# Sending the expert gates of twenty chunks through DRAM in transposed form, inside a fused attention and mixture-of-adapters kernel

## The chip, the cores and the metric

The kernel runs on one NeuronCore of one Trainium2 chip. The metric is the device time of one execution in microseconds, as the median of repeated runs. A separate execution was taken by the hardware profiler; its own time and its span are given below, and every duration quoted from a row or a trace is from that one execution.

The engines are TensorE (PE, with its weight loads shown apart as PEld), VectorE (DVE), ScalarE (ACT), GpSimd (POOL) and SyncE (SP). SP computes nothing here: it only issues DMAs, in program order. POOL also issues one kind of DMA, the query casts.

## The reference

Attention over spatially pooled keys feeds a top-2 mixture of low-rank adapters, applied to every token:

```
kv_pool = kv.reshape(B, H//4, 4, W//4, 4, C).mean(axis=(2, 4))   # 768 keys per batch
k = v = kv_pool.reshape(B, -1, C) @ w_sr
x = softmax(q @ k.T / sqrt(C)) @ v          # B = 4, 12288 queries each, C = 128
logits = x @ w_gate                         # 8 experts
w = softmax over the two largest logits of each token, 0 for the other six
out = x + sum over experts e of  w[e] * ((x @ A[e]) @ B[e])      # rank 16
```

The eight adapters together are one 128x128 matrix on the way down (8 experts times rank 16) and one on the way up. The gate of an expert multiplies its 16 rank columns between the two.

## The kernel before, in words

The 49152 tokens are cut into 96 chunks of 512 (24 chunks per batch), and four chunks make a group that shares one query load. Inside a chunk, S = 4 blocks of 128 tokens are handled side by side. All engines run from one order written by hand: the start and the last 24 chunks are literal lists of steps, and chunks 14 to 71 come from `slot(k)`, which emits the steps of one slot. Each engine executes its own instructions strictly in that order, so the place of a step in a slot is also its place in the engine's queue.

A chunk passes through a slot pipeline. In slot k:

- `sc k 0..2` computes the scores of chunk k, three times two 128x512 matmuls, and ACT takes the exponential of each pair (`em`).
- `at k-1 0..3` multiplies chunk k-1's exponentials with the values: four blocks of six matmuls into `acc`. The values carry the gate logits and a row sum as extra columns.
- `nm k-2` (DVE: reciprocal, then one multiply) normalizes into `xn`; `tp k-2` takes the sorted top logits (four MAX8); `ro` lets POOL work out the tanh argument and the top-2 mask for a pair of chunks.
- `ga k-4`, once per pair: ACT's tanh, then two POOL operations give the gates `gw` of both chunks, laid out tokens by experts.
- `tt k-6 k-7`: eight 128x128 transposes on PE into one PSUM tile, four of them of chunk k-6's normalized output, four of chunk k-7's gated product `hg`; one DVE copy brings all eight to SBUF (`tts`).
- `dn k-6`: four 128-column matmuls with the transposed output as weights give the down projection with tokens on partitions, and `ge k-6` multiplies it by `gw` on DVE, which expands each gate over its 16 rank columns in the access pattern.
- `up k-8`, `fi k-8`: the up projection from the transposed `hg`, the addition of the attention output on DVE, and the output DMA on SP.

Other work is laid in between: `pr` and `pa` prepare the keys and values of the next batch (PE and DVE in `pr`, POOL in `pa`), `kv` loads it (SP), `lq` (SP) loads the transposed queries of a group by a DMA transpose, and `cq` (POOL) casts a later group's queries to bf16 from DRAM to DRAM. `lq` must wait for its cast. `cq` begins with a one-element copy `late` that reads the previous group's `qT`, so a cast does not start before that load has landed.

PSUM is fully used: `sg` two buffers of two banks, `acc` one of two banks, and `mb` two buffers of one bank that `tt`, `dn`, `up` and `pr` take in turn.

The lines that matter in the profile: line 68 is the helper that records every matmul, line 79 the cast, line 84 the DMA transpose, 319 the exponential, 333 and 337 the normalization, 367 the MAX8, 380 to 386 the routing, 392 to 395 the gates, 416 the copy after the transposes, 430 the gate product, 443 and 444 the addition and the output DMA, 606 the `late` copy.

Of the kernel before, what the change touches and what calls it, by code (L numbers as in the profile page):

```python
# [10 lines left out]
FP32 = mybir.dt.float32  # L11
BF16 = mybir.dt.bfloat16
U16 = mybir.dt.uint16
FP16 = mybir.dt.float16
AF = mybir.ActivationFunctionType
ALU = mybir.AluOpType
# [4 lines left out]
def kernel(  # L21
# [10 lines left out]
    nc = tc.nc  # L32
    P = 128
    B, N, C = q.tensor.shape
    E, RK = 8, 16
# [3 lines left out]
    T = 512  # L39
    S = T // P  # L40
    GC = 4
    GT = GC * T
# [6 lines left out]
    const = ctx.enter_context(tc.tile_pool(name="const", bufs=1))  # L49
# [6 lines left out]
    rpool = ctx.enter_context(tc.tile_pool(name="rpool", bufs=4))  # L56
    gpool = ctx.enter_context(tc.tile_pool(name="gpool", bufs=6))
    run = ctx.enter_context(tc.tile_pool(name="run", bufs=3))
    opool = ctx.enter_context(tc.tile_pool(name="opool", bufs=6))
    qdram = ctx.enter_context(tc.tile_pool(name="qdram", bufs=1, space=bass.MemoryType.DRAM))  # L60
    ps_s = ctx.enter_context(tc.tile_pool(name="ps_s", bufs=2, space=bass.MemoryType.PSUM))
    ps_a = ctx.enter_context(tc.tile_pool(name="ps_a", bufs=1, space=bass.MemoryType.PSUM))
# [2 lines left out]
    keep = tc.keep_in_program_order  # L65

    def mm(*a, **k):
        return keep(nc.tensor.matmul(*a, **k))  # L68

    def mtile(shape, dtype=FP32, name="mb"):  # L70
        return ps_m.tile(shape, dtype, tag="mb", name=name)


    NG = N // GT
    q_bf, qT, kvr = {}, {}, {}

    def cast_q(g):
        t = qdram.tile([GT, C], BF16, tag=f"q{g}", name=f"qbf{g}")
        keep(nc.gpsimd.dma_start(t, q[g // NG, (g % NG) * GT:(g % NG + 1) * GT]))
        q_bf[g] = t  # L80

    def load_qT(g):
        t = qpool.tile([P, GT], BF16, tag="qT", name="qT")
        keep(nc.sync.dma_start(t.rearrange("c (j p) -> c j p", p=P),
                               q_bf[g].rearrange("(p j) c -> p (j c)", p=P), transpose=True))
        qT[g] = t


# [34 lines left out]
    for item in """  # L123
# [5 lines left out]
        at = [None if x == "-" else int(x) for x in at]  # L129
# [13 lines left out]
    id_f = const.tile([P, P], FP32)  # L143
# [24 lines left out]
    def one(pool):  # L168
        if pool == "mb":
            return mtile([P, T], name="tail_ps")  # L170
        if pool == "acc":
            return ps_a.tile([P, S, 256], FP32, tag="acc", name="acc").rearrange(
                "p a c -> p (a c)")[:, 0:T]
        return ps_s.tile([P, 2, T], FP32, tag="sg", name="sg")[:, 0]

    def move(engine, o, i):
        return keep(nc.scalar.copy(o, i) if engine == "A" else nc.vector.tensor_copy(o, i))
# [129 lines left out]
    em, acc, xn, xg, srt, gw = {}, {}, {}, {}, {}, {}  # L307
    tts, xT, hgT, hp, hg, dp = {}, {}, {}, {}, {}, {}
# [34 lines left out]
    def normalize_half(k, h):  # L343
        if ("r", k) not in xn:
            xn["r", k] = rpool.tile([P, S], FP32, tag="rinv", name="rinv")
        if k // GC not in xg:
# [5 lines left out]
            xn[k][:, 2 * h:2 * h + 2], a[:, :, 0:VC],  # L352
            ri.unsqueeze(2).broadcast_to([P, 2, VC]), op=ALU.mult)))

    sizes = [1, 1] + [2] * (NB * (B - 1) // 2 - 1) + [1] * NB
    first, size = {}, {}
    for n in sizes:
        k0 = len(first)
# [3 lines left out]
    def top(k):  # L362
        k0, m = first[k], k - first[k]
        if k0 not in srt:
            srt[k0] = rpool.tile([P, GC, S, 8], FP32, tag="srt", name="srt")
        for s in range(S):
            keep(nc.vector.max(srt[k0][:, m, s], xn[k][:, s, C:VC]))  # L367

# [2 lines left out]
    def route(k0):  # L371
        n = size[k0] * S
        eng = nc.gpsimd
        m0 = k0 % GC * S
        lg = xg[k0 // GC].rearrange("p m s c -> p (m s) c")[:, m0:m0 + n, C:VC]
        so = srt[k0].rearrange("p m s e -> p (m s) e")[:, 0:n]

        def over(i):
            d = rpool.tile([P, GC * S, 8], FP32, tag=f"over{i}", name=f"over{i}")[:, 0:n]
            keep(eng.tensor_tensor(  # L380
                d, lg, so[:, :, i].unsqueeze(2).broadcast_to([P, n, 8]), op=ALU.subtract))
            return d

        arg, mask = over(0), over(1)
        keep(eng.tensor_tensor(arg, arg, mask, op=ALU.add))  # L385
        keep(eng.tensor_scalar(mask, mask, 0.0, None, op0=ALU.is_ge))  # L386
        routed[k0] = (n, eng, arg, mask)

    def gates(k0):
        n, eng, arg, mask = routed[k0]  # L390
        th = rpool.tile([P, GC * S, 8], FP32, tag="th", name="th")[:, 0:n]
        keep(nc.scalar.activation(th, arg, AF.Tanh, bias=0.0, scale=0.5))  # L392
        w = gpool.tile([P, GC * S, 8], FP32, tag="gw", name="gw")
        keep(eng.tensor_tensor(w[:, 0:n], th, mask, op=ALU.mult))  # L394
        keep(eng.tensor_tensor(w[:, 0:n], w[:, 0:n], mask, op=ALU.add))
        gw[k0] = w
# [30 lines left out]
    def gate(k):  # L427
        k0, m = first[k], k - first[k]
        hg[k] = run.tile([P, S, P], BF16, tag="hg", name="hg")
        keep(nc.vector.tensor_tensor(  # L430
            hg[k].rearrange("p s (e r) -> p (s e) r", e=E),
            hp[k].rearrange("p s (e r) -> p (s e) r", e=E),
            gw[k0][:, m * S:(m + 1) * S].rearrange("p s e -> p (s e)")
            .unsqueeze(2).broadcast_to([P, S * E, RK]), op=ALU.mult))

    def up(k):
        dp[k] = mtile([P, S, C], name="d_ps")
        for s in range(S):
            mm(dp[k][:, s], hgT[k][:, s], b_bf, start=(s == 0), stop=(s == S - 1))
# [153 lines left out]
    a_bf = const.tile([P, P], BF16)  # L593
    b_bf = const.tile([P, C], BF16)

    def adapters():
        keep(nc.vector.tensor_scalar(a_bf, a_f, 0.5, None, op0=ALU.mult))
        keep(nc.vector.tensor_copy(b_bf, b_f))

    def first_casts(watch):  # L600
        keep(nc.gpsimd.tensor_copy(late, watch))
        for g in range(2, 4):
            cast_q(g)

    def next_cast(g):
        keep(nc.gpsimd.tensor_copy(late, qT[g - 1][:, 0:1]))
        cast_q(g)
# [3 lines left out]
    def plan(b):  # L611
# [8 lines left out]
        "k2": project_k, "va": project_v, "vb": copy_v, "tu": turn_v,  # L620
        "cs": lambda w: first_casts(q_f[1][:, 15, 0:1]),
        "cab": adapters,
        "lq": load_qT, "cq": next_cast,
        "kv": lambda b, h, r: load_kv(b, h, r, None),
        "pa": lambda b, n: plan(b)[0][n // 8][n % 8](),
        "pr": lambda b, n: plan(b)[1][n](),
        "sc": scores, "at": attend, "nm": normalize, "tp": top, "ro": route, "ga": gates,
        "tt": lambda x, h, e: transposes(x, h, nc.scalar if e == "A" else nc.vector),
        "dn": down, "up": up,
        "ge": lambda k: gate(k) if len(hp[k].shape) == 3 else gate_part(k, 0, S),  # L630
        "fi": lambda k: finish(k) if len(dp[k].shape) == 3 else add_here(k, 0, S),
        "nh": normalize_half, "xb": hold_x, "xt": turn_x, "cx": fetch_x, "hb": hold_h, "ht": turn_h, "ch": fetch_h,
        "o95": hold_acc, "pt": attend_part, "hd": hold_hp, "dn2": down_into, "ge2": gate_part,
        "db": hold_d, "up2": up_part, "af": add_here, "ca": carry, "pd": add_there,
        "lastroute": route_here, "lt": tanh_here, "lg_": gates_here,
    }

    def follow(order):
# [7 lines left out]
    def slot(k):  # L646
        b, i = divmod(k, NB)
        o = []
        if k % GC == 0 and k // GC + 1 < B * NG:
            o.append(f"lq {k // GC + 1}")  # L650
        i0 = 4 if b == 0 else 0
        if b + 1 < B and i0 <= i < i0 + 12:
            o.append(f"kv {b + 1} {(i - i0) // 4} {(i - i0) % 4}")
        if k % GC == 2 and k // GC + 2 < B * NG:
            o.append(f"cq {k // GC + 2}")
        o.append(f"sc {k} 0")
        if first[k - 4] == k - 4:
            o.append(f"ga {k - 4}")
        o += [f"nm {k - 2}", f"tt {k - 6} {k - 7} V", f"sc {k} 1", f"up {k - 8}", f"fi {k - 8}",
              f"at {k - 1} 0", f"tp {k - 2}"]  # L660
        if first[k - 2] + size[k - 2] - 1 == k - 2:
            o.append(f"ro {first[k - 2]}")
        o += [f"sc {k} 2", f"dn {k - 6}", f"ge {k - 6}"]
        prs = (14, 15, 16, 18, 19, 20, 21, 22, 23) if b == 0 else (11, 12, 13, 17, 18, 19, 21, 22, 23)
        if b + 1 < B and i in prs:
            o.append(f"pr {b + 1} {prs.index(i)}")
        o += [f"at {k - 1} {s}" for s in range(1, S)]
        if b + 1 < B and i % 2 == 0 and (8 if b == 0 else 6) <= i <= 20:
            lo, n = ((0, 3, 7, 10, 14, 17, 21)[(i - 8) // 2], 4 if i % 4 else 3) if b == 0 else (
                (i - 6) // 2 * 3, 3)  # L670
            o += [f"pa {b + 1} {m}" for m in range(lo, lo + n)]
        return "; ".join(o)
# [119 lines left out]
```

The softmax here doesn't subtract the row's maximum and nothing guards it: scores larger than these inputs give would overflow.

## Time and profile before

| | us |
|---|---|
| median of 9 runs | 389.12 (389.03 to 389.47) |
| the profiled execution | 389.18 |
| its span | 387.4 |
| PE busy in the span | 374.4 (97%) |
| DVE busy | 313.5 (81%) |
| ACT busy | 308.5 (80%) |
| POOL busy | 211.4 (55%) |

The granted TensorE clock is full in all 40 slices of the span. A slot of the loop lasts about 3.6 us, longer where `pr` adds its matmuls; slot 34 begins at 142.30 us of the span, slot 36 at 149.83, slot 40 at 164.99. Busy time of PE is modelled from pipelined matmuls, so 97% by itself does not say how close PE is to its peak; the order of the matmuls in time does.

### The profile page before, as it was taken

The page shows a single profiled execution, that of the slowest core. Times are in us where ns is not written, and L with a number is a line of the kernel's source. Part 1 is how long each engine was busy: PE and PEld are TensorE (multiplying, and loading weights), DVE is VectorE, ACT ScalarE, POOL GpSimd, SP SyncE. Part 2 cuts the span into 40 slices and gives each one's busy share as a digit, 9 for nine tenths or more (in the row PEclk, how much of TensorE's full clock was granted, in tenths as well). Part 3 has the DMA queues.
Part 4 walks back from the last instruction along what each step waited for, and adds up shares of the span by engine and source line. Part 5 has one row for each costly group of instructions (what it writes and reads, how often), then busy time and mean ns, then how long its engine had stood idle before and what let it go on. Part 6 is the DMA issues. An engine that isn't in the chain of part 4 may idle for free.

```text
span 387.4 us, 11738 instructions
## 1 busy us (share of the span) xinstructions
PE 374.4 (97%) x4546; PEld 303.6 (78%) x4620; DVE 313.5 (81%) x973; ACT 308.5 (80%) x401; POOL 211.4 (55%) x474
## 2 busy tenths in 40 slices
PE   7999999999999999999999999999999999999994
PEld 4867888888888888888888888888877778788893
DVE  1445688989888888988988889888877687988896
ACT  1688997777687787877778778786879999998964
POOL 0011868988331777867433586877613234545682
PEclk9999999999999999999999999999999999999999
DMA  7998986985599999675589989855744676532245
GB/s 269 408 267 198 310 208 200 267 183 139 136 257 240 322 251 278 152 182 139 116 198 253 319 203 341 190 138 143 159 110 90 135 143 179 111 95 104 78 165 219
DMA packets 70744, 76.47 MB, mean 197 GB/s; under 512 B 49856, under 2 KB 51392, under 8 KB 70336
## 3 DMA queue, kind: packets, MB, share of 16 engines
q1 hardware_dynamic: 69552, 63.98, 54.4%
q0 software_dynamic: 704, 11.54, 17.1%
q8 instruction: 36, 0.59, 0.6%
q10 hardware_dynamic: 432, 0.20, 0.2%
q14 instruction: 20, 0.16, 0.2%
HBM read 50.53 MB, written 36.70 MB: 225 GB/s over the span
## 4 chain that ended last, share of the span: by engine, by line
PE 80%; DMA 6%; POOL 5%; DVE 3%; ACT 2%; issue 2%; SPq 0%; POOLq 0%; DVEq 0%; ACTq 0%
PE acc L68 32%; PE sg L68 25%; PE tt_ps L68 9%; DMA kvr<-in_kv_dram 6%; PE h_ps L68 5%; PE d_ps L68 4%; PE tail_ps L68 3%; ACT em L319 2%; POOL osb L562 1%; PE v_ps L68 1%; POOL over L380 1%; DVE rinv L333 1%; PE kpT_ps L68 1%; POOL gw L394 1%; POOL over L385 1%
## 5 line engine op out<-in xcount | busy, mean ns | idle before, releaser
L319 ACT ACTIVATE em<-sg 128x1024 f16<-128x1024 f32 x288 | 278.4, 1026 | 56.6 <-PE sg L68 42.4
L68 PE MATMUL acc<-vx,em 128*128 128x137 f16 x2280 | 168.9, 223 | 0.4
L68 PEld LDWEIGHTS <-em 128*128 128x128 f16 x2304 | 147.3, 98 | 11.4 <-DVE xn L337 2.7
L68 PE MATMUL sg<-qT,kfT 128*128 128x512 bf16 x502 | 154.0, 379 | 0.1
L68 PEld LDWEIGHTS <-tts 128*128 128x128 bf16 x660 | 49.2, 98 | 31.8 <-issue 0.4
L264 POOL TENSOR_TENSOR kvr<-kvr 128x512 f32<-128x512 f32 x54 | 67.5, 1273 | 0.0
L337 DVE TENSOR_TENSOR xn<-acc,rinv 128x544 f32<-128x544 f32 x83 | 60.1, 724 | 3.2 <-DVE rinv L333 0.3
L380 POOL TENSOR_TENSOR over<-xn,srt 128x64 f32<-128x64 f32 (+1 forms) x114 | 29.9, 284 | 54.6 <-DVE srt L367 54.4
L416 DVE COPY tts<-tt_ps 128x1024 bf16<-128x1024 bf16 (+1 forms) x83 | 53.9, 651 | 4.8 <-PE tt_ps L68 4.6
L394 POOL TENSOR_TENSOR gw<-th,over 128x64 f32<-128x64 f32 (+1 forms) x57 | 16.8, 294 | 68.2 <-ACT th L392 67.3
L68 PEld LDWEIGHTS <-kfT 128*128 128x128 bf16 x576 | 46.1, 98 | 2.8
L430 DVE TENSOR_TENSOR hg<-h_ps,gw 128x512 bf16<-128x512 f32 x58 | 40.1, 691 | 4.5
L68 PEld LDWEIGHTS <-xn 128*128 128x128 bf16 x384 | 28.7, 98 | 18.2
L443 DVE TENSOR_TENSOR osb<-d_ps,xn 128x512 f32<-128x512 f32 x58 | 40.1, 691 | 0.0
L333 DVE RECIPROCAL rinv<-acc 128x4 f32<-128x4 f32 x83 | 15.1, 182 | 29.0 <-PE acc L68 28.4
L68 PE MATMUL tt_ps<-id_bf,xn 128*128 128x128 bf16 x344 | 33.2, 219 | 0.9
L367 DVE MAX8 srt<-xn 128x8 f32<-128x8 f32 x368 | 33.0, 152 | 0.1
L68 PE MATMUL tt_ps<-id_bf,hg 128*128 128x128 bf16 x316 | 30.4, 219 | 0.0
L68 PEld LDWEIGHTS <-hg 128*128 128x128 bf16 x384 | 25.7, 98 | 2.0 <-DVE hg L531 0.3
L68 PE MATMUL h_ps<-a_bf,tts 128*128 128x128 bf16 x264 | 25.5, 219 | 1.1
L68 PE MATMUL d_ps<-b_bf,tts 128*128 128x128 bf16 x260 | 25.1, 219 | 0.8
L386 POOL TENSOR_SCALAR over<-over 128x64 f32<-128x64 f32 (+1 forms) x57 | 19.2, 337 | 5.2
(119 smaller groups left out, 324.4 us busy)
## 6 DMA issues: line engine op xcount, KB each, us to landing
out_dram<-osb SPq DMA_DIRECT2D x91, 256.0 KB, 3.1
kvr<-in_kv_dram SPq DMA_DIRECT2D x45, 512.0 KB, 6.0
qbf<-in_q_dram POOLq DMA_DIRECT2D x22, 512.0 KB, 6.3
kvr<-in_kv_dram SPq DMA_DIRECT2D x6, 256.0 KB, 8.9
out_dram<-osb SPq DMA_DIRECT2D x9, 128.0 KB, 2.3
qf<-in_q_dram SPq DMA_DIRECT2D x4, 256.0 KB, 7.4
qf<-in_q_dram SPq DMA_DIRECT2D x2, 512.0 KB, 7.8
qT<-qbf SPq DMA_TRANSPOSE x22, 5.4
```

Of the source, the lines that this page charges most:

```text
L68: return keep(nc.tensor.matmul(*a, **k))
L264: keep(nc.gpsimd.tensor_tensor(u[:, lo:hi], u[:, lo:hi], v[:, lo:hi], op=ALU.add))
L319: keep(nc.scalar.activation(em[k][:, 2 * r:2 * r + 2], ps, AF.Exp, bias=0.0, scale=scale))
L333: keep(nc.vector.reciprocal(ri, acc[k][:, :, VC]))
L337: keep(nc.vector.tensor_tensor(x, acc[k][:, :, 0:VC], ri.unsqueeze(2).broadcast_to([P, S, VC]), op=ALU.mult))
L367: keep(nc.vector.max(srt[k0][:, m, s], xn[k][:, s, C:VC]))
L380: keep(eng.tensor_tensor(d, lg, so[:, :, i].unsqueeze(2).broadcast_to([P, n, 8]), op=ALU.subtract))
L386: keep(eng.tensor_scalar(mask, mask, 0.0, None, op0=ALU.is_ge))
L394: keep(eng.tensor_tensor(w[:, 0:n], th, mask, op=ALU.mult))
L416: keep(nc.vector.tensor_copy(sb[:, lo:hi], ps[:, lo:hi]))
L430: keep(nc.vector.tensor_tensor(hg[k].rearrange("p s (e r) -> p (s e) r", e=E), hp[k].rearrange("p s (e r) -> p (s e) r", e=E), gw[k0][:, m ...
L443: keep(nc.vector.tensor_tensor(osb, dp[k], xn[k][:, :, 0:C], op=ALU.add))
```

## The change

For the chunks in `turned` (30 to 41 and 54 to 61: twenty chunks, ten pairs) the gated product is made directly in its transposed form, so that it needs no transposes on PE.

- `ga` writes the gates of the pair in fp16 into one of three 128x128 tiles (`wide`), experts before blocks, instead of `gw`.
- `g1`, late in slot k0+4 for the pair that begins at k0: one PE transpose of that tile (128 columns, so with 64 unused ones) into an `mb` buffer, and a 64x128 DVE copy. `g2` writes the result to DRAM from SP (16 KB).
- `g3`, in the middle of slot k0+5: SP loads it back over all 128 partitions, each expert's row read 16 times, once for each rank (256 KB).
- In slot k+7, a turned chunk k has its output transposed (`tt k -`, four transposes and a 128x512 copy, one slot later than before), then `dT`: one 128x512 matmul with the adapter matrix as weights, which gives the down projection with ranks on partitions; `gT` multiplies it by the loaded gates on DVE and the product goes to `up` as it is.
- The casts: source and destination are cut into 128 runs, 4 KB each in the destination, and the DRAM tile's rows are 4352 bytes apart instead of 4096; before, a cast was 16 rows of 16384 elements. This holds for all 22 casts.
- At the start, `adapters` also copies an fp16 identity and clears the three `wide` tiles on DVE.

The slot at which each range begins loses the `tt`, `dn` and `ge` work of its first chunk, and the slot after each range (48, 68) has both kinds.

```diff
 def cast_q(g):
-        t = qdram.tile([GT, C], BF16, tag=f"q{g}", name=f"qbf{g}")
-        keep(nc.gpsimd.dma_start(t, q[g // NG, (g % NG) * GT:(g % NG + 1) * GT]))
+        t = qdram.tile([P, (S * GC + 1) * C], BF16, tag=f"q{g}", name=f"qbf{g}")[:, 0:S * GC * C]
+        keep(nc.gpsimd.dma_start(
+            t, q[g // NG, (g % NG) * GT:(g % NG + 1) * GT].rearrange("(p j) c -> p (j c)", p=P)))
...
+    turned = {*range(30, 42), *range(54, 62),}
+    id_h = const.tile([P, P], FP16)
+    wide = [const.tile([P, P], FP16, name=f"wide{i}") for i in range(3)]
...
         keep(nc.scalar.activation(th, arg, AF.Tanh, bias=0.0, scale=0.5))
-        w = gpool.tile([P, GC * S, 8], FP32, tag="gw", name="gw")
+        if k0 in turned:
+            keep(eng.tensor_tensor(th, th, mask, op=ALU.mult))
+            gh[k0] = wide[k0 // 2 % 3]
+            keep(eng.tensor_tensor(
+                gh[k0][:, 0:n * E].rearrange("p (e m) -> p m e", e=E), th, mask, op=ALU.add))
+            return
...
+    def turn_gates(k0, pool, engine):
+        n = size[k0] * S * E
+        ps = one(pool).bitcast(FP16)[:, 0:P]
+        mm(ps, gh[k0], id_h, is_transpose=True, start=True, stop=True)
+        gt[k0] = rpool.tile([P, P], FP16, tag="gt", name="gt")[0:n]
+        move(engine, gt[k0], ps[0:n])
+
+    def put_gates(k0):
+        gd[k0] = gdram.tile([E, size[k0] * T], FP16, tag=f"gd{size[k0]}", name="gd")
+        keep(nc.sync.dma_start(gd[k0].rearrange("e (m t) -> (e m) t", t=P), gt[k0]))
+
+    def spread_gates(k0):
+        n = size[k0] * T
+        gx[k0] = gxpool.tile([P, GC // 2 * T], FP16, tag="gx", name="gx")[:, 0:n]
+        keep(nc.sync.dma_start(gx[k0], gd[k0].unsqueeze(1).broadcast_to([E, RK, n])))
+
+    def down_turned(k, pool):
+        hp[k] = one(pool)
+        mm(hp[k], a_bf, xT[k].rearrange("p s t -> p (s t)"), start=True, stop=True)
+
+    def gate_turned(k):
+        m = k - first[k]
+        hgT[k] = run.tile([P, S, P], BF16, tag="hg", name="hg")
+        keep(nc.vector.tensor_tensor(hgT[k].rearrange("p s t -> p (s t)"), hp[k],
+                                     gx[first[k]][:, m * T:(m + 1) * T], op=ALU.mult))
...
     def adapters():
...
+        keep(nc.vector.tensor_copy(id_h, id_f))
+        for t in wide:
+            keep(nc.vector.memset(t, 0.0))
...
-        o += [f"nm {k - 2}", f"tt {k - 6} {k - 7} V", f"sc {k} 1", f"up {k - 8}", f"fi {k - 8}",
-              f"at {k - 1} 0", f"tp {k - 2}"]
+        o.append(f"nm {k - 2}")
+        far, near = k - 7 in turned, k - 6 not in turned
+        x = k - 6 if near else "-"
+        h = "-" if k - 7 in turned else k - 7
+        if (x, h) != ("-", "-"):
+            o.append(f"tt {x} {h} V")
+        if far:
+            o.append(f"tt {k - 7} - {'A' if near else 'V'}")
+        o.append(f"sc {k} 1")
...
-        o += [f"sc {k} 2", f"dn {k - 6}", f"ge {k - 6}"]
+        o.append(f"sc {k} 2")
+        if far:
+            o += [f"dT {k - 7} mb", f"gT {k - 7}"]
+        if near:
+            o += [f"dn {k - 6}", f"ge {k - 6}"]
...
-        o += [f"at {k - 1} {s}" for s in range(1, S)]
+        o.append(f"at {k - 1} 1")
+        if first[k - 5] == k - 5 and k - 5 in turned:
+            o.append(f"g3 {k - 5}")
+        o.append(f"at {k - 1} 2")
+        if first[k - 4] == k - 4 and k - 4 in turned:
+            o += [f"g1 {k - 4} mb V", f"g2 {k - 4}"]
+        o.append(f"at {k - 1} {S - 1}")
```

## The prediction

> **What bounds the kernel now.** I read the page first: PE is busy for 374.4 of 387.4 us and the clock row is 9 in every slice, so no time is lost to the clock. Since PE's busy time is modelled, I then took the chain that ended last in order of time, in the middle of the part that changes. This is slot 39 (start us, length us, what):
>
> ```profile
> 161.34 0.43 PE sg L68 x2
> 161.78 0.45 PE tt_ps L68 x8
> 162.22 0.43 PE sg L68 x2
> 162.65 0.22 PE d_ps L68 x4
> 162.88 0.36 PE acc L68 x6
> 163.24 0.43 PE sg L68 x2
> 163.67 0.22 PE h_ps L68 x4
> 163.89 1.09 PE acc L68 x18
> ```
>
> Each piece starts where the one before ends, so the slot (161.34 to 164.99) is exactly the sum of its matmuls: 0.45/8 = 0.0556 us for 128 columns, 0.433/2 = 0.2165 for 512. PE issues without a gap; in this part of the kernel a matmul taken away is time taken away, for as long as nobody else becomes late. So the next question is how much air the others have. The timeline of the same slot on VectorE (the bracket is idle time before it, and what ended it):
>
> ```profile
> 161.38 0.18 DVE L333 RECIPROCAL rinv<-acc 128x4 f32<-128x4 f32 x1 [0.32 <-PE acc L68]
> 161.60 0.72 DVE L337 TENSOR_TENSOR xn<-acc,rinv 128x544 f32<-128x544 f32 x1
> 162.26 0.69 DVE L416 COPY tts<-tt_ps 128x1024 bf16<-128x1024 bf16 x1
> 162.91 0.69 DVE L443 TENSOR_TENSOR osb<-d_ps,xn 128x512 f32<-128x512 f32 x1
> 163.52 0.36 DVE L367 MAX8 srt<-xn 128x8 f32<-128x8 f32 x4
> 163.93 0.69 DVE L430 TENSOR_TENSOR hg<-h_ps,gw 128x512 bf16<-128x512 f32 x1
> 165.01 0.18 DVE L333 RECIPROCAL rinv<-acc 128x4 f32<-128x4 f32 x1 [0.39 <-PE acc L68]
> ```
>
> It works 3.24 us of 3.65 and then waits 0.39 for PE. ScalarE is busy 2.9 to 3.1 us a slot. Both follow PE with 0.4 us or more to spare.
>
> **What it removes and adds on PE.** Per turned chunk, four transposes of `hg` and four matmuls of `dn` go; one 512-column matmul comes; per pair, one 128-column gate transpose comes. For twenty chunks: 160 x 0.0556 = 8.90 us out, 20 x 0.2165 = 4.33 and 10 x 0.0556 = 0.56 in: **minus 4.01 us**. The four transposes of the output move one slot and cost the same, so the lighter slots 36 and 60 and the heavier 48 and 68 cancel. [...]
>
> **What the others get.** A turned slot is 3.65 - 0.22 = 3.43 us, 3.48 with the gate transpose. VectorE's copy after the transposes falls from 128x1024 (691 ns) to 128x512 (418 ns in the 128x512 row of the same line); the product from PSUM stays at 0.69 (a float32 source of 128x512; fp16 gates in place of float32 ones have no row: between 0.69 and, if the second source helped, about 0.42 as in the bf16 copy; I take 0.69). The 64x128 copy of `g1` has no row either: between MAX8's 152 ns and the 292 of the 128x128 float32 copy; 0.2. That is 3.24 - 0.27 = 2.97 a slot, 3.17 with `g1`: less than PE in both. In the three `pr` slots with values (36, 42, 60) VectorE has 0.43 + 0.41 more and PE 0.52: about 4.0 to 3.95 plus. There it runs some 0.1 to 0.25 us late. What is late next is `nm`, then `at 0`, which needs `acc` free: `nm` ends 0.93 after the slot's start and `at 0` stands at 0.43 + 0.22 + 0.43 + 0.22 = 1.31, so 0.3 is absorbed. Slots 48 and 68 use the two `mb` buffers five times instead of three, behind an ACT copy of 0.585; I put 0.15 each on them. In sum **plus 0.3** for VectorE and the ring. ScalarE: 3 x 1.02 + 0.25 = 3.2 at most, under 3.43; nothing. `adapters` (0.22 + 3 x about 0.1) stands before an idle 1.22 us of VectorE at 36.5 to 38.05 us; nothing, and 0.5 us if that idle time is gone.
>
> **The new wait on POOL.** Before, the gates had two slots of air. Now `g1` wants them on PE in the same slot. POOL's queue in slot 34, which begins at 142.30:
>
> ```profile
> 142.66 0.19 POOL L606 CAST late<-qT 128x1 f32<-128x1 bf16 x1
> 142.79 0.58 POOL L79 DMA_DIRECT2D qbf<-in_q_dram  x1
> 144.15 0.32 POOL L394 TENSOR_TENSOR gw<-th,over 128x64 f32<-128x64 f32 x1 [0.78 <-ACT th L392]
> 144.55 0.32 POOL L395 TENSOR_TENSOR gw<-gw,over 128x64 f32<-128x64 f32 x1
> ```
>
> The gates end 2.57 us into the slot, and the tanh, not POOL, sets this. `g1` comes at 3.04 us into the shortened slot (the pieces above, less 0.22, up to the last six `acc`). Air: 0.47 us. Behind `g1` on PE stand the last six `acc` matmuls, so every nanosecond beyond that stops everything. In slots 34, 38, 42, 58 and 62 the cast stands ahead of the gates. It goes from 32 packets (704 over 22 casts) to at least 128; its issue is 0.58 us now. Bounds: no more than now, or four times, 2.34 us. The second would use the idle 0.78, the 0.47, and cost 1.76 - 1.25 = 0.5 us in five slots, 2.5 in all. The nearest row is the instruction's own, 0.51 to 0.76 us over the 22 casts, and I stay nearer to it than to the fourfold: 1.0, and nothing lost.
>
> **The new wait on the gates' way through DRAM.** `gT` stands on VectorE's queue, and `g1`, `nm` and the next copy stand behind it. From the start of slot k0+4: the gate copy ends at about 3.5, `g2` issues in 0.35 and lands 1.9 to 3.0 after (least and median of output DMAs), so at about 6.2; `g3` issues only then, and SP's outputs wait behind it, with six buffers to spare. Outputs of 256 KB land in 3.0 us median: 9.3. `gT` of the first chunk is due in slot k0+7 at 3 x 3.45 + 2.56 = 12.9. [...] What can stand ahead on SP is the query load:
>
> ```profile
> SPq L84 <- DMA qbf<-in_q_dram: 40.0, 14, 9.5
> ...
> qT<-qbf SPq DMA_TRANSPOSE x22, 5.4
> ```
>
> (the waits of SP's queue: us, times, longest; and the page's DMA row, us to landing). It waits for its cast in 14 of 22 cases. [...] In slots 34, 35, 58 and 59 the last key loads share the queue; there slots 36 and 60 are 0.5 longer through their values. So I cost the DMAs at nothing in most pairs and put **plus 0.3** for one or two late ones.
>
> **The casts.** A 16 KB packet takes 0.171 x 387.4 x 16 / 704 = 1.5 us of an engine, a 4 KB one about 0.4. Others get in between, which shortens their way, and the cast itself gets slower: from 5.9 us median by up to some 2 us where the queues are full. Then `lq` waits longer. It is due one group, four slots, later: 4 x 3.45 - 2.5 - 5.4 = 5.9 us of air. The next cast's `late` copy has less (in slot 38 the load should land near 157.0 and `late` ran at 157.96): a cast later by over 1 us makes POOL wait, and the gates have 1.2 us for that. No cost taken, 1 to 2 us if it goes wrong.
>
> **The sum.** -4.01 + 0.3 + 0.3 = -3.4. The profiled execution took 389.18, 1.78 around a span of 387.40; nothing changes around the span. 389.18 - 3.4 = 385.8; the median of the runs is 0.06 lower: **385.7 us**, 0.9% faster.
>
> **The rivals.**
> 1. The gain comes through but for a part: `g1` waits for POOL behind longer casts (2.5), or late `lq` and `late` copies (1 to 2). 386.7 to 388.2, at 387.5. For it: five slots with only 0.47 us of air. Against: the tanh sets the gates there, with 0.78 idle.
> 2. Slower: `g3` lands late in every pair. Price: from `g2` issued at 3.6 and landed at 6.2 a `g3` of 8 us ends at 14.3, 1.4 after it is due; 0.3 is absorbed, 1.1 is lost in each of ten pairs: 389.1 - 3.7 + 11 = 396. The gain is gone from 3.7/10 + 0.3 = 0.67 us of lateness, that is from a landing of 7.4 us. For it: output DMAs landed in up to 9.4 us and key loads in up to 10.2. Against: between 160 and 188 us the DMA engines are busy only 0.4 to 0.7 on most stretches, as the key loads are over by 150.
> 3. No change: VectorE or ScalarE becomes the bound and PE waits in the freed time. It would need 3.65 us of work in a slot; the rows give 3.17. 389.1.
> 4. More: PE's gain as counted, none of the small losses, and finer casts that unblock the start: 385.0 to 384.7.
>
> **How the numbers follow.** Forecast (385.2 to 386.5) 0.60, rival 4 0.07, rival 1 0.16, rival 3 0.04, rival 2 0.13. A change of 0.2%, 0.8 us, is about what a measurement of this kernel can tell from none (its nine runs spread over 0.44). Rival 1 lies almost wholly below 388.3, so faster 0.82, same 0.05, slower 0.13. The range leaves out rival 2, rival 3 and the edges: 384.8 to 388.2.
>
> **What would show it.** In the chain of turned slots `tt_ps x4`, one 0.22 matmul for `dT`, slots of 3.43 and 3.48 us, no wait of PE for POOL and none of VectorE for `gx`; still `rinv` waiting for `acc`. The prediction is wrong if the waits list VectorE behind DMA `gx` or weight loads behind POOL `wide`, if the cast's issue is above 1.8 us, or if `lq` waits push `late`.

## The result, and the profile after

The changed kernel takes **392.91 us** (median of 10 runs, 390.14 to 399.0) against 389.06 for the kernel before (31 runs, 388.61 to 389.57): a ratio of 1.0092 (95% interval 1.0079 to 1.0105). It is 3.9 us slower. The prediction of 385.7 us, faster, was wrong.

The profiled execution of the changed kernel took 396.83 us (span 395.0) and was granted a TensorE clock of 0.50 from 259.7 to 266.5 us, so I use it to see where things wait, not for the size of the loss; the same waits stand in the traces of e2, e11 and e12 below, whose mean granted clock is 0.997, 0.999 and 0.997. Medians and ranges in this document are of all the runs counted beside them, while the ratios leave out the few slow ones.

The half-clock stretch begins just behind the longest wait for the gates (4.4 us, over at 259.58). In e15's chain the matmuls take nearly twice their time behind a wait of 3.5 us, over at 255.80 (twelve of `acc` 1.38 us at 258.80, for 0.72 at 241.91); behind a wait of 4.2 us in e12's, over at 168.28, they do not (0.72 at 171.05). What lowers the clock is not shown by these runs.

The page of the changed kernel (busy time by engine; DMA queues with packets, MB, share of 16 engines; the new gate product with count, busy us, mean ns, idle before it):

```profile
PE 377.4 (96%) x4418; PEld 301.4 (76%) x4490; DVE 309.7 (78%) x987; ACT 309.8 (78%) x403; POOL 212.0 (54%) x474
...
q1 hardware_dynamic: 71712, 66.76, 56.0%
q0 software_dynamic: 3168, 11.54, 17.6%
...
L472 DVE TENSOR_TENSOR hg<-tail_ps,gx 128x512 bf16<-128x512 f32 x20 | 13.8, 691 | 12.4 <-DMA gx<-gd 9.9
```

PE has 128 matmul records fewer than before (130 by the count; some records can be missing), and is busier all the same: the stretch at half clock adds to it (5.94 us busy for 38 matmuls), and part of its waiting seems to count as busy: the record of one 128-column transpose is 220 ns long, where eight in a row take 0.45 us. The new product costs 691 ns, as assumed, and VectorE stood idle 9.9 us before it for the gates. The waits name the same place (us in all, times, longest):

```profile
DVE hg L472 <- DMA gx<-gd: 9.9, 4, 4.4
POOL late L648 <- DMA qT<-qbf: 6.2, 5, 1.8
PEld L70 <- DVE hg L472: 4.9, 2, 3.4
PEld L70 <- POOL wide L403: 0.8, 1, 0.8
```

The first line is what the prediction named as its own refutation. The chain that ended last, in order of time (start, length, what), shows the shape of the three longest waits: gates' write, gates' load, product.

```profile
155.91 3.52 DMA gd<-gt
...
159.44 6.48 DMA gx<-gd
...
166.01 0.69 DVE hg L472
...
172.47 3.32 DMA gd<-gt
...
175.81 6.20 DMA gx<-gd
...
182.10 0.70 DVE hg L472
...
248.93 2.27 DMA gd<-gt
...
251.22 8.27 DMA gx<-gd
...
259.58 0.69 DVE hg L472
```

I had counted 2.6 us for the write and 4.5 for the load. Here they take 2.3 to 3.5 and 6.2 to 8.3. Why is seen in the two timelines around the first of them. SP:

```profile
152.29 2.90 SPq L87 DMA_TRANSPOSE qT<-qbf  x1
...
155.91 0.53 SPq L458 DMA_DIRECT2D gd<-gt  x1
...
159.44 0.63 SPq L463 DMA_DIRECT2D gx<-gd  x1
160.17 0.39 SPq L483 DMA_DIRECT2D out_dram<-osb  x1
161.11 0.51 SPq L458 DMA_DIRECT2D gd<-gt  x1
```

and POOL (in brackets the idle time before, and what ended it):

```profile
158.79 0.19 POOL L648 CAST late<-qT 128x1 f32<-128x1 bf16 x1 [1.71 <-DMA qT<-qbf]
159.03 0.61 POOL L81 DMA_DIRECT2D qbf<-in_q_dram  x1
...
160.06 0.48 POOL L403 TENSOR_TENSOR wide<-th,over 128x64 f16<-128x64 f32 x1
```

The query load of slot 36 stands in front of the gates' write; its landing lets the next cast go at 159.03, and the gates' load is issued at 159.44, behind that cast. What moved in the DMA engines from 160.2 to 163.4 us (the DMA view of that stretch):

```profile
DMA packets 112, 0.46 MB, mean 143 GB/s; under 512 B 0, under 2 KB 0, under 8 KB 112
...
q0 software_dynamic: 112, 0.46, 95.2%
```

Only the cast. The gates' load and an output had been issued on SP's queue before or at the start of these 3.2 us, the next gates' write within them, and not one packet of theirs began.

As a common measure for the experiments I add up, from the starts of `rinv` in the traces, slots 34 to 49 and 58 to 69, in us. The stretch between them (slots 50 to 57, outside the change) is 29.02 or 29.03 in all of these kernels.

| kernel | 34 to 49 | 58 to 69 | sum | longest slots |
|---|---|---|---|---|
| before | 60.76 | 45.61 | 106.37 | 4.15 (`pr` with values) |
| after | 63.30 | 51.02 | 114.32 | 5.40, 5.22; 7.27, 5.36 |
| e3, casts alone | 60.75 | 45.61 | 106.36 | 4.15 |
| e1, no gates | 61.43 | 45.92 | 107.35 | 5.34; 4.73 |
| e6, no gates, no POOL wait | 59.64 | 44.73 | 104.37 | 4.06 |
| e7, e6 and the ring | 59.22 | 44.46 | 103.68 | 4.34 |
| e13, later start, casts elsewhere | 59.87 | 44.92 | 104.79 | 4.15 |
| e14, casts in their slots | 59.87 | 45.81 | 105.68 | 5.13 |

In after, slot 64 (5.36 us) and the first part of slot 65 (4.25) lie in the half-clock stretch, which makes up about 2.5 us of its sum: 5.36 against 3.34 in slot 40, 4.25 against 3.71 in slot 41.

### The profile page after: what moved, and what is told of

The parts are those of the page before. It is cut to its first block, busy times and chain, and to the rows that moved or that the text cites. A ratio compares the mean times of both kernels' runs of the same rounds, so it can differ in the third digit from the quotient of the medians.

```text
span 395.0 us, 11539 instructions
## 1 busy us (share of the span) xinstructions
PE 377.4 (96%) x4418; PEld 301.4 (76%) x4490; DVE 309.7 (78%) x987; ACT 309.8 (78%) x403; POOL 212.0 (54%) x474
## 4 chain that ended last, share of the span: by engine, by line
PE 68%; DMA 16%; DVE 5%; POOL 5%; ACT 3%; issue 2%; SPq 0%; POOLq 0%; DVEq 0%; ACTq 0%
PE acc L70 28%; PE sg L70 21%; PE tt_ps L70 7%; DMA gx<-gd 7%; DMA kvr<-in_kv_dram 6%; PE tail_ps L70 4%; DMA gd<-gt 4%; PE d_ps L70 3%; PE h_ps L70 3%; ACT em L322 2%; POOL osb L601 1%; POOL over L387 1%; DVE rinv L336 1%; DVE xn L340 1%; PE v_ps L70 1%
## 5 line engine op out<-in xcount | busy, mean ns | idle before, releaser
L70 PE MATMUL acc<-vx,em 128*128 128x137 f16 x2280 | 171.0, 224 | 1.1 <-DVE xn L340 0.7
L70 PEld LDWEIGHTS <-em 128*128 128x128 f16 x2304 | 149.0, 98 | 14.8 <-DVE xn L340 4.2
L70 PEld LDWEIGHTS <-tts 128*128 128x128 bf16 x500 | 36.9, 98 | 22.4 <-issue 0.4
L429 DVE COPY tts<-tt_ps 128x1024 bf16<-128x1024 bf16 (+1 forms) x83 | 47.8, 578 | 5.1 <-PE tt_ps L70 4.9
L407 POOL TENSOR_TENSOR gw<-th,over 128x64 f32<-128x64 f32 (+1 forms) x47 | 13.6, 290 | 57.0 <-ACT th L399 56.1
L443 DVE TENSOR_TENSOR hg<-h_ps,gw 128x512 bf16<-128x512 f32 x38 | 26.3, 691 | 2.7
L472 DVE TENSOR_TENSOR hg<-tail_ps,gx 128x512 bf16<-128x512 f32 x20 | 13.8, 691 | 12.4 <-DMA gx<-gd 9.9
L70 PE MATMUL tt_ps<-id_bf,hg 128*128 128x128 bf16 x236 | 22.6, 219 | 0.0
L392 POOL TENSOR_TENSOR over<-over,over 128x64 f32<-128x64 f32 (+1 forms) x57 | 16.7, 294 | 4.5
```

The costliest lines, as they stand in the source:

```text
L429: keep(nc.vector.tensor_copy(sb[:, lo:hi], ps[:, lo:hi]))
L443: keep(nc.vector.tensor_tensor(hg[k].rearrange("p s (e r) -> p (s e) r", e=E), hp[k].rearrange("p s (e r) -> p (s e) r", e=E), gw[k0][:, m ...
```

## The experiments

Diffs are against the changed kernel and show the lines that matter ("..." marks what is left out); times are medians with (lowest to highest, runs), ratios are to the kernel before, run beside each. Where two runs are compared, the ratios and their intervals decide.

### The casts alone, and the casts as they were

e3 turns no chunk:

```diff
-    turned = {*range(30, 42), *range(54, 62),}
+    turned = set()
```

> The change with an empty set of turned chunks: only the casts in 4 KB runs (and the few start instructions) remain. Theory A: query loads have 6 us of air and the casts are hidden: within 0.5 of before, 388.8 to 389.6. Rival D, the casts cost: 391 or more.

388.77 us (388.57 to 389.53, 10), ratio 0.9993 (0.9982 to 1.0005). The 4 KB casts by themselves cost nothing and gain nothing, and in e3's slots nothing differs from before. e2 keeps the turned chunks and puts the old casts back:

```diff
-        t = qdram.tile([P, (S * GC + 1) * C], BF16, tag=f"q{g}", name=f"qbf{g}")[:, 0:S * GC * C]
-        keep(nc.gpsimd.dma_start(
-            t, q[g // NG, (g % NG) * GT:(g % NG + 1) * GT].rearrange("(p j) c -> p (j c)", p=P)))
+        t = qdram.tile([GT, C], BF16, tag=f"q{g}", name=f"qbf{g}")
+        keep(nc.gpsimd.dma_start(t, q[g // NG, (g % NG) * GT:(g % NG + 1) * GT]))
...
-                               q_bf[g], transpose=True))
+                               q_bf[g].rearrange("(p j) c -> p (j c)", p=P), transpose=True))
```

> The changed kernel with the casts as they were (16 rows of 16384 elements). Theory A: a cast holds all DMA engines for about 3 us in either form and the gates still wait behind it, so still slower than before: 391 to 393, at most 1.5 better than the change since a cast in large pieces takes some 0.5 to 1 us less. Rival D, the casts in 4 KB runs are what costs: 385.5 to 387.

397.39 us (395.47 to 397.99, 4), ratio 1.0209 (1.018 to 1.0237): 4.5 us more than after. I had expected no such help from the finer casts. e2's trace has more of both waits, for the query load and for the gates, than after (6.2 and 9.9):

```profile
POOL late L647 <- DMA qT<-qbf: 17.2, 8, 4.3
DVE hg L471 <- DMA gx<-gd: 12.6, 7, 2.7
```

A cast in its old form holds the engines too: from 162 to 165 us, with a gates' load and an output issued, only its packets, of some 32 KB each, began:

```profile
q0 software_dynamic: 13, 0.43, 87.1%
```

With the turned chunks the new casts are worth having; the loss lies in the turned chunks. The edit takes back two things at once, the 4 KB runs and the rows 4352 bytes apart, and no run tells them apart.

### The gates left out

e1 multiplies by a constant tile of ones instead of the loaded gates; the gates are still turned, written and loaded.

```diff
-                                     gx[first[k]][:, m * T:(m + 1) * T], op=ALU.mult))
+                                     g_one, op=ALU.mult))
...
```

> The changed kernel, but the twenty turned products read a tile of ones that is written once at the start; the gates are still transposed, written to DRAM and loaded back, and nobody reads them (so the gates are left out of the result of these chunks). Theory A, the gates' way through DRAM is late and VectorE waits for it, and the freed PE time is real: all of the loss goes and the time is that of the count, about 385.2 to 386.0, with no wait of VectorE for the gates. Rival B, the DMAs themselves or the longer casts disturb other work (late query loads, POOL): the time stays above 389. Rival C, PE does not get its time back since VectorE, ScalarE or POOL bind: 388 to 389.5 with no wait for the gates.

388.59 us (386.91 to 390.92, 10), ratio 0.999 (0.9971 to 1.0009). So 4.3 us of the medians (1.0% by the ratios, 4.0 us) is VectorE's wait for the gates, more than the whole loss; but the gain of 4 us is not there even so. Two things remain. e1's waits:

```profile
POOL late L650 <- DMA qT<-qbf: 9.4, 7, 2.7
...
PEld L70 <- POOL wide L404: 3.0, 2, 1.8
...
PE tail_ps L70 <- POOL wide L404: 2.6, 2, 1.6
```

and a turned slot in its chain:

```profile
165.69 0.43 PE sg L70 x2
166.12 0.22 PE tt_ps L70 x4
166.35 0.43 PE sg L70 x2
166.78 0.22 PE d_ps L70 x4
167.00 0.36 PE acc L70 x6
167.36 0.53 PE sg L70 x2
167.89 0.22 PE tail_ps L70
168.10 0.72 PE acc L70 x12
168.82 0.06 PE tail_ps L70
168.88 0.36 PE acc L70 x6
169.24 0.43 PE sg L70 x2
```

First, twice (slots 38 and 62) PE waits for `wide`: `late` waits 2.7 us for a query load and the gates stand behind it on POOL. That query load comes late because it stands in SP's queue behind the gates' load of the pair before, which waits for its own write to land:

```profile
152.48 0.70 SPq L464 DMA_DIRECT2D gx<-gd  x1
153.36 2.87 SPq L87 DMA_TRANSPOSE qT<-qbf  x1
```

In before the same query load was issued at 151.55. Second, the third score pair takes 0.53 instead of 0.43, in every turned slot. It writes the PSUM buffer that the slot's first exponential reads. From the first score pair to the third there are now 167.36 - 165.69 = 1.67 us, where before it was 163.24 - 161.34 = 1.90. ScalarE shows what the pair waits for:

```profile
166.22 1.02 ACT L322 ACTIVATE em<-sg 128x1024 f16<-128x1024 f32 x1 [0.64 <-PE sg L70]
```

The exponential ends at 167.24 and the pair can start only after it; in the trace its matmuls begin at 167.30. The work taken out of a slot was taken out between two users of a buffer. ScalarE has idle time, but not there.

### The two remaining waits, taken away one at a time

All three keep e1's tile of ones. e5 moves the 512-column matmul ahead of the third score pair, which gives the 0.22 us back to the exponential:

```diff
-        o.append(f"sc {k} 2")
         if far:
             o += [f"dT {k - 7} mb", f"gT {k - 7}"]
+        o.append(f"sc {k} 2")
```

> As the run with the tile of ones (gates left out of the turned chunks, their DMAs kept), with the turned down projection and its product placed before the third score pair instead of after it. Theory A2, what is left of the loss there is 0.1 us in each turned slot, in which the third score pair waits for ScalarE to free its PSUM buffer, since 0.22 us of transposes between the first pair and the third are gone: twenty slots less 0.1, so 1.5 to 2 us better than that run, 386.5 to 387.2. If ScalarE's buffers do not matter: no change from it, 388.6.

e6 lets the five casts near the turned slots go without waiting for the query load before:

```diff
     def next_cast(g):
-        keep(nc.gpsimd.tensor_copy(late, qT[g - 1][:, 0:1]))
+        if g not in (10, 11, 12, 16, 17):
+            keep(nc.gpsimd.tensor_copy(late, qT[g - 1][:, 0:1]))
         cast_q(g)
```

> As the run with the tile of ones (gates left out of the turned chunks), but the five casts that are issued in slots 34, 38, 42, 58 and 62 no longer wait for the previous group's query load. Theory A3, POOL stalls on that wait since the query load is late, and the gate transpose then stops PE (2.6 us in two places): 385.5 to 387 and no wait of PE for the gates of POOL. If the transposes' wait has another cause: 388 to 389.

e7 has both.

> Both edits of the two runs beside it, on the run with the tile of ones (gates left out). If the three losses are all there is (the gates' load, ScalarE's buffer, POOL's wait), the count of PE's matmuls is left: 384.8 to 385.5. If something else binds, 386 or more.

| | us | ratio |
|---|---|---|
| e5 | 390.08 (387.38 to 391.76, 9) | 1.0029 (1.0002 to 1.0057) |
| e6 | 386.98 (386.4 to 395.22, 10) | 0.9962 (0.9933 to 0.999) |
| e7 | 386.21 (385.81 to 393.48, 4) | 0.993 (0.9914 to 0.9947) |

In e6 and e7 the waits of PE for POOL are gone. In the table above the sum falls by 2.98 from e1 to e6 (the two long slots are 1.8 and 1.2 of it). The medians fall by 1.6 and the ratios by 0.28% (1.1 us), but the intervals of e1 and e6 overlap, and so do those of e6 and e7, so what each wait cost by itself is shown by the traces and not by the times. Both together are clear of the scatter: from e1 to e7 the ratio falls by 0.6% (2.3 us). e5 missed its number: its slots became shorter as expected, but the POOL waits stayed (slots of 4.86 and 4.23) and its runs scatter. In e7 a plain turned slot is 3.40 us, 3.45 with the gate transpose, where the prediction counted 3.43 and 3.48. e7's chain, with the two steps changed over:

```profile
168.16 0.36 PE acc L70 x6
168.52 0.22 PE tail_ps L70
168.74 0.43 PE sg L70 x2
```

The score pair is back at 0.43. In the slots with both kinds of chunk (48 and 68) the change of place costs: 4.34 and 4.33 against 4.06. There ScalarE copies the turned chunk's transposed output, behind its tanh in slot 48, and the 512-column matmul, now earlier, waits for that copy. In e7's chain of slot 48:

```profile
194.62 0.48 ACT tts L428
195.10 0.04 issue
195.15 0.38 PE tail_ps L70
```

That is why the ring is worth 0.7 us in the slots from e6 to e7 and not the 2 us of 20 times 0.1: twelve slots gain 0.09 each, those with `pr` 0.05 or less, and the two mixed slots lose 0.55 together. Slot 45 is 4.06 us long in e7, where 0.22 less than before would be 3.68: there PE's weight load waits for POOL's `kvr` (0.7 us, once).

### The gates again: order, ranks, one more slot

Can the gates come in time? e4 puts, from slot 34 to 47 and 58 to 67, the query load behind the gates' write on SP, and the cast at the end of its slot on POOL:

```diff
+        moved = 34 <= k < 48 or 58 <= k < 68
-        if k % GC == 0 and k // GC + 1 < B * NG:
+        if k % GC == 0 and k // GC + 1 < B * NG and not moved:
...
+        if moved and k % GC == 0:
+            o.append(f"lq {k // GC + 1}")
+        if moved and k % GC == 2:
+            o.append(f"cq {k // GC + 2}")
         o.append(f"at {k - 1} {S - 1}")
```

> The changed kernel with two steps moved in slots 34 to 47 and 58 to 67: the query load stands after the gates' write on SP (instead of ahead of it), and the cast stands at the end of its slot, behind the gates on POOL. Theory A: the chain that fails is query load waiting for its cast, the gates' write behind it, and the load of the gates then behind the next cast; with the order turned the gates of the pairs that begin at multiples of four go ahead of both: 385.5 to 387.5, with no more than 1 us of waits for the gates. If the wait comes from the slowness of the loads themselves (8 source rows, each read 16 times) wherever they stand: 389.5 to 392.

390.24 us (389.04 to 391.55, 10), ratio 1.0032 (1.0019 to 1.0045). 2.7 us better than after (2.3 by the ratios), not the gain I expected: VectorE's wait for the gates fell from 9.9 to 4.4 us in four waits, and POOL's `late` grew from 6.2 to 9.8, since a later load makes the next cast later.

e12 is the complete kernel with e5's and e6's edits together, e8 is e12 with the five casts issued in slots 19, 20, 21, 47 and 49, well before the turned slots:

```diff
+        ahead = {19: 10, 20: 11, 21: 12, 47: 16, 49: 17}
-        if k % GC == 2 and k // GC + 2 < B * NG:
+        if k % GC == 2 and k // GC + 2 < B * NG and k // GC + 2 not in ahead.values():
             o.append(f"cq {k // GC + 2}")
+        if k in ahead:
+            o.append(f"cq {ahead[k]}")
```

> The complete computation: the changed kernel with the turned down projection before the third score pair and the five casts free of their wait; the gates' way is as in the change. From the runs with ones the first two are worth about 2 and 2 to 3 us; what is left of the loss is the wait for the gates: about 388 to 390, with 3 to 8 us of waits for the gates in the trace.

> The complete computation: the changed kernel with the turned down projection before the third score pair, and with the five casts that fall among the gates' DMAs issued earlier (in slots 19, 20, 21, 47 and 49) and without waiting for a query load. Theory A: no cast holds the DMA engines while gates are on their way, so VectorE waits less than 1 us in all for them: 385.0 to 386.5, faster than before. If the loads are late by themselves: 388 to 391.

e12: 395.06 us (391.44 to 399.28, 4), ratio 1.0125 (1.0069 to 1.0181). e8: 390.38 us (388.19 to 392.94, 6), ratio 1.005 (1.0013 to 1.0087). Both missed. e12 is not better than after, whose ratio lies in its interval: shorter slots do not help by themselves; its trace has 8.0 us of waits for the gates. In e8 only the first pairs are late. Its chain:

```profile
146.39 6.66 DMA gd<-gt
...
153.06 3.92 DMA gx<-gd
```

The load is quick now, and the 16 KB write took 6.66 us. What lies beside it there are the key loads of slots 34 and 35 and a query load in SP's queue. So the casts are not the only thing in the way. That the key loads are, no run tests by itself.

e15 tells the round trip from the load: e12, with `dT` ahead of the third score pair only where a slot has no old chunk, and the load reading a tile of ones in DRAM that was written at the start, so that it need not wait for the gates' write.

```diff
-        keep(nc.sync.dma_start(gx[k0], gd[k0].unsqueeze(1).broadcast_to([E, RK, n])))
+        keep(nc.sync.dma_start(gx[k0], gd0.unsqueeze(1).broadcast_to([E, RK, n])))
...
```

> The complete change with the score order and the freed casts (as in the run ring_free), but the gates' load reads a DRAM tile of ones that was written once at the start; the gates are still written to DRAM and nobody reads them there (so the gates are left out of the turned chunks). The load no longer waits for the write: if the round trip is what makes the gates late, the waits for the load vanish but for 0.5 us: 386 to 387. If a load by itself is late, behind a cast: 389 to 392, with pieces of 4 to 8 us of load left in the chain.

387.86 us (386.03 to 391.89, 10), ratio 0.9967 (0.9946 to 0.9988), between the two expectations. By the ratios e15 is 1.6% (6 us) faster than e12, and the wait of the load for the write is worth most of that (the slots 48 and 68 also gain the few tenths named above); the load alone can still be late. Its trace has two of 7.9 and 8.9 us, each issued within 0.02 us of a cast. Here the engines were shared: from 158.5 to 163.5 us 135 packets of the cast and 255 of SP's queue began, 66.6% and 23.6% of the engines' time.

e9 is e12 with every turned chunk one slot later (`dT` in slot k+8, `up` in k+9). e10 is e9, and e11 is the changed kernel, with the gates' load in rank order (16 in front instead of 8, the adapters' ranks reordered to match). The run that e10 is held against is e9.

```diff
-        far, near = k - 7 in turned, k - 6 not in turned
+        far, near = k - 8 in turned, k - 6 not in turned
...
-        if k - 8 in turned:
-            done.insert(0, k - 8)
+        if k - 9 in turned:
+            done.insert(0, k - 9)
```

```diff
-        keep(nc.sync.dma_start(gx[k0], gd[k0].unsqueeze(1).broadcast_to([E, RK, n])))
+        keep(nc.sync.dma_start(gx[k0], gd[k0].unsqueeze(0).broadcast_to([RK, E, n])))
...
```

> The complete computation: the changed kernel with the turned down projection before the third score pair, the five casts free of the wait for a query load, and every turned chunk one slot later (its transposes, down projection and product in slot k+8, its up projection in k+9). Theory A: the gates are late by 0.2 to 4.4 us, and 3.45 us more covers nearly all of it: 385.3 to 386.8, VectorE waits less than 1 us for gates. If lateness grows with the slack (the DMA queue is overfull): 388 or more.

> [...] Theory A: the load is no more on the path: same as that run within 0.5. [...]

> [...] Theory A, the time of the load is waiting behind a cast or behind other transfers in the queue: little better, 391.5 to 393, and pieces of 4 to 8 us remain.

| | us | ratio |
|---|---|---|
| e9 | 389.26 (388.51 to 393.53, 10) | 1.0031 (1.0002 to 1.0061) |
| e10 | 389.43 (388.48 to 393.22, 10) | 1.0025 (0.9998 to 1.0052) |
| e11 | 393.37 (390.09 to 395.71, 4) | 1.0107 (1.0052 to 1.0162) |

e9 has no wait for the gates that counts (one of 0.2 us), and missed its number nonetheless: the later chunks pile up behind each range, where slots 48 and 49 take 4.34 and 4.35 and slots 68 and 69 take 4.34 and 5.23, against 3.63 and 3.63, and 3.63 and 3.90, before. That eats the gain. The rank order makes no difference that these runs can tell, in either kernel: e11's chain has loads of 3.5 to 6.2 us, where after's has 4.9 to 8.3. How many engines a load had is not in the profile, so what the order does to that is not shown.

### A version that beats both kernels

e13 begins the first range four chunks later, behind the key loads (34 to 41 and 54 to 61, sixteen chunks), sends the casts of groups 11, 12, 16 and 17 without waiting in slots 20, 21, 47 and 49, and moves `dT` ahead of the third score pair only in slots without an old chunk. e14 is the same with those four casts in their old slots, not waiting either.

```diff
-    turned = {*range(30, 42), *range(54, 62),}
+    turned = {*range(34, 42), *range(54, 62),}
...
+        ahead = {20: 11, 21: 12, 47: 16, 49: 17}
...
-        o.append(f"sc {k} 2")
+        if near:
+            o.append(f"sc {k} 2")
         if far:
             o += [f"dT {k - 7} mb", f"gT {k - 7}"]
+        if not near:
+            o.append(f"sc {k} 2")
```

> The complete computation: chunks 34 to 41 and 54 to 61 turned (30 to 33 no longer, so that no gates travel while the key loads of slots 24 to 35 do), the turned down projection before the third score pair where only turned chunks are in the slot, and the four casts of slots 38, 42, 58 and 62 issued in slots 20, 21, 47 and 49. Sixteen chunks are worth 3.2, the two mixed slots cost 0.4: 386.2 to 387.0 if key loads and casts were what made the gates late, and no more than 0.5 us of waits for them. If the round trip is too long by itself: 388.5 or more.

> As the run beside it, with the four casts in their slots 38, 42, 58 and 62 (not waiting for a query load). If the casts are what makes the gates late: 2 to 5 us slower than that run, 388.5 to 391.5, with 2 us or more of waits for the gates. If it was the key loads alone: within 0.5 of it.

e13: **386.65 us** (386.54 to 387.63, 4), ratio **0.9944** (0.993 to 0.9959), faster than before by 2.4 us and as expected. e14: 391.27 us (388.54 to 398.85, 5), ratio 1.0061 (1.0006 to 1.0116). The two differ in where four casts are issued, and in nothing else. The intervals do not overlap, and the ratios differ by 1.2% (4.6 us). e13's chain at its latest load:

```profile
246.37 2.40 DMA gd<-gt
...
248.78 4.50 DMA gx<-gd
```

and e14's at the same pair:

```profile
245.06 2.15 DMA gd<-gt
...
247.22 6.93 DMA gx<-gd
```

The write is as short, the load 2.4 us longer with a cast issued at 246.50, just ahead of it. The query load before it on SP is issued 3.65 us ahead of the write in e13 and 4.15 in e14, so it is not what holds the load. e14's profiled execution was its quickest (388.54), so its trace shows the mechanism and less than the median's loss. e13's trace still has 1.9 us of VectorE waiting for the gates, in two waits, more than I expected: in the second range the write takes 6.47 us at 235.39, where the key loads of slots 58 and 59 share the queue.

## Why the prediction was wrong, step by step

- **What bounds the kernel** (PE's matmuls, end to end): right. With the waits gone a plain turned slot is as long as its matmuls: 3.40 and 3.45 us in e7 against 3.43 and 3.48 counted.
- **PE: minus 4.01.** The price of a slot was right. No run shows the whole: e7's trace is 2.69 below before in the two stretches (3.4 in its span, 384.0 against 387.4), and the other 1.3 went in the slots 48 and 68 (0.48 each beyond 3.63 + 0.22) and 45 (0.38). The rows of 0.0556 and 0.2165 us were the right price.
- **VectorE and the ring: plus 0.3.** VectorE's price was right: 0.69 for the product. The slots 48 and 68 were counted as 0.22 heavier and given 0.15 each on top; they went from 3.63 to 4.06, so 0.21 on top, and by another 0.27 in e7's order.
- **"ScalarE: 3 x 1.02 + 0.25 = 3.2 at most, under 3.43; nothing."** This step failed too, though it was not what turned the sign. It compared totals of a slot. ScalarE's time is enough, but the third score pair needs the first exponential's buffer, and taking the `dn` and transposes away moved that pair from 1.90 to 1.67 us behind the first. 0.1 us in a turned slot, 0.7 to 0.8 us in what e7's order could take back.
- **The new wait on POOL: nothing.** The cast's issue cost nothing, as taken: 606 ns at the median, for 585 before, where the working allowed 1.0 us. But it was the smaller of two dangers in that place, and the other decided. `late`, named in the step on the casts as 1 to 2 us, "if it goes wrong", with no cost taken, did go wrong: 3.0 us in the slots of e1's trace. The reason taken for it, a slower cast, was not the one: the query load is issued some 2 us later (153.36 for 151.55) behind the gates' load on SP, in slots 0.2 shorter, and so holds `late`, and with it the gates.
- **"The new wait on the gates' way through DRAM": plus 0.3.** This is the step that turned the sign: taking the wait away (e1) gave back 4.0 us by the ratios, where 0.3 was counted, an estimate for one or two late pairs that no run shows. It took 2.6 us for the write, from the rows of output DMAs, and 4.5 for the load, my estimate between two rows of the page before (256 KB outputs 3.1 us to landing, 512 KB key loads 6.0), in whose place the chains show 3.9 to 8.9; and it found no cast on the way: it asked what the casts do to POOL and to `lq`, not what they do to the gates. In after the two take 9.5 to 10.5 us together where VectorE waits longest, of the 7.1 taken. Beside a cast the late loads of after, e14 and e15 take 6.2 to 8.9 us; e13 against e14 shows the cast as cause. The long writes of e8 (6.7 us) and e13 (6.5), with no cast under way, stand beside key loads, which points to a second cause. It was also told as all or nothing: a forecast with one or two late pairs, or rival 2 with all ten. The trace has four waits in ten pairs, the longest 4.4 us.
- **The casts: "Others get in between, which shortens their way".** Not seen where the gates were late in after: from 160.2 to 163.4 us nothing got in between the 4 KB packets, 112 of them at 95.2% of the engines' time. That packets cut finer let the others in was my estimate. In e2's trace the old cast, in packets of 32 KB, held the engines in the same way (13 packets, 87.1%, from 162 to 165 us); e15, where both queues moved together for 5 us (135 packets of the cast, 255 of SP's queue), shows that a cast need not hold all of them. What decides between the two no run shows, and which engine had which packet is not in the profile. The packet size in the working was wrong: a row of 16384 elements is 32 KB in bf16, and in before, from 173 to 177 us, 16 packets of a cast move its 0.52 MB; the other 16 of its 32 carry next to nothing. A slower cast was not seen either. The page of before has 6.3 us to landing at the median (the working's 5.9 is of casts and query loads together), that of e3, where only the casts are changed, 5.8, and that of after 7.2.
- **The order of the gates' load:** no gain. The shortest loads in the chains take 3.9 us with the experts in front (e8, e13) and 3.5 in rank order (e11), but neither kernel with the rank order (e10, e11) is faster than the one without.
- **The rivals.** Rival 1 held for POOL and `late`, rival 2's mechanism for part of the pairs; the median lies between their times. Together they had 0.29, and slower, at 0.13, was too low. The range ended at 388.2 because it left rival 2 out whole.
- **`adapters`: nothing.** Nothing in any trace speaks against it.

Left open: why e12, with both small waits removed, is no better than after (its gates are as late, which its trace shows, but not why the removal of one wait feeds the other), what the key loads cost by themselves, and how much of the scatter of the runs comes from the gates' landing.

## What to carry to other kernels

A small dependent pair of DMAs in a busy kernel is priced by what can stand before it in its queue and by what holds the engines when it is issued, not by the landing time of other transfers of its size (here 16 KB took 2.2 to 7.6 us and 256 KB 3.5 to 8.9); list the large transfers that are issued within its time and move those first. When work is taken out of a tight loop, check the spacing between each two users of a rotating buffer (here 1.67 us for 1.90), and not only the totals of the engines. A wait that lets one transfer start when another lands ties their queues together, so a small delay goes round: here query load (in e1 at 153.36 us for 151.55), cast, gates, and the next load.

## What the hardware showed that I had not expected

- A cast from DRAM to DRAM (512 KB in its destination, 128 runs of 4 KB) kept the engines to itself in after: in the 3.2 us from 160.2 to 163.4 its 112 packets were the only ones that began, at 95.2% of the engines' time, while transfers on the other queue waited. In e15, where a load was issued in the same moment, the two queues shared them (66.6% and 23.6%).
- All the same the 4 KB runs are worth 4.5 us in the changed kernel (e2 against after) and nothing with no turned chunks (e3). Why is open: a cast holds the engines in either form (95.2% and 87.1%), but with the old one `late` waited 17.2 us and VectorE 12.6, for 6.2 and 9.9.
- 128 runs in place of 16 rows cost POOL next to nothing to issue: 606 ns against 585 at the median.
- A write of 16 KB took from 2.2 us (e14) to 7.6 (e2) from issue to where its load could go; the long ones stand beside casts and key loads.
